# One token tile moved from packed weights to a DMA transpose, and weight pruning by halves, in a 2:4 sparse matmul

## The chip, the cores and the metric

The kernel runs on one core of a Trainium2 chip. The metric is the device time of one execution in microseconds. A profile of one execution lies beside it; times inside it count from the first instruction of its span.

## What is computed

```python
B, S, D = 16, 512, 1024
wg = w.reshape(D // 4, 4, D)                 # groups of 4 rows
mag = abs(wg)
thr = second largest of the 4 magnitudes     # per group and column
mask = (mag >= thr)
wp = (wg * mask).reshape(D, D)               # 2:4 pruned weights
out = einsum("bsd,df->bsf", x, wp) + b       # x is 8192 x 1024, all bf16
```

So the weights are pruned first, two kept of each four rows in a column, and a product of 8192 x 1024 by 1024 x 1024 follows, with a bias.

## The kernel before

**Tiles.** The 8192 tokens are 64 tiles of 128. The product of one tile is 16 matmuls of TensorE (PE) that are 512 columns wide: 8 blocks of 128 input rows by 2 halves of the output columns (h = 0 and 1). `g` = 0 and 1 are the first and the last 512 input rows.

**Weights in pieces.** The weights are loaded in six pieces, numbered from 0: pieces 0 to 3 are 256 columns each of the first input half (g = 0), pieces 4 and 5 are 512 columns each of the second. A partition holds four consecutive rows of the weights, one group, so pruning needs no exchange between partitions. `abs_piece` (L109) makes magnitudes, on VectorE (DVE) except for piece 3, which ScalarE (ACT) does; `prep_piece` (L124) makes maxima and minima of pairs, the threshold, the mask (L150) and the product with the weights (L153). Pieces 0 to 2 do mask and product by halves (two of the four rows each): in pieces 1 and 2 both masks come first, then both products. Piece 3 and later ones take one mask and one product.

**Two ways to use the weights.** While they are still in this *packed* layout, a matmul can read them if the tokens' columns are permuted to match. The first `T` = 8 tiles do so for the first input half: `load_x` (L76) loads half a tile, `transpose_half` (L177) transposes it on PE by four matmuls of 128 columns (L182), `copy_half` (L184, L187) brings it from PSUM to SBUF. These tiles can start on each piece as soon as it is pruned. For the second input half their tokens come transposed by DMA (tile `xg`, L324). All other tiles are transposed wholly by DMA and read the weights in natural order (`wp_nat`), which `unpack` (L170) makes by four DMAs for each piece of 512 columns once it is pruned. The `F` = 6 tiles behind the packed ones are the *fill* tiles: two DMA transposes (L259), one for each input half, bring them to `xfill`; they give PE work between the pieces. The rest comes in batches, one of 2 tiles and then six of 8 (L266).

**The order by hand.** The first part is a string of steps, `FRONT` (L285), and the program keeps the written order on each engine. A step is a letter and numbers:

- `A.i`, `P.i`: magnitudes, then pruning, of piece i.
- `T.t`, `C.t`: PE transpose and ACT copy of packed tile t.
- `M.i.t`: piece i for packed tile t, four matmuls, one for each row m of the groups. `N.i.t.m...` is the same for the listed m alone, so that a half piece can be used. They are 256 columns wide for pieces 0 to 3 and 512 for 4 and 5 (L203).
- `X.q.t`: a fill tile, q = 2g + h, four matmuls of 512 (L203). `Y.t`: a fill tile's h = 1, all eight (L263).
- `V.h.t`: ACT moves a finished half sum to a stage in SBUF (L235). `O.h.t`: DVE adds the second half sum to it (L239). `B`, and the loop's `add_bias`: DVE adds the bias (L243). `evac_dve` (L248) does it straight from PSUM.
- `I`, `D.g`, `G`, `U.g.h`, `Q`, `L.n`: on SP's DMA queue a load of weights, a fill transpose of half g, the transpose to `xg`, an unpack, the bias, a batch's transpose. SP issues them in the order in which they are written.

PSUM has 8 banks, given out in turn (L53), so a sum waits until the one that had its bank has been moved. `later` (L343) holds the stage halves whose bias is added in the main loop, which does the 50 batch tiles (L359).

Of the kernel before, what the change touches and what calls it, by code (L numbers as in the profile page):

```python
# [10 lines left out]
def kernel(  # L11
# [8 lines left out]
    P = 128  # L20
# [7 lines left out]
    B, S, D = x.shape  # L28
# [7 lines left out]
    xf = x.flatten_outer_dims()  # L36
    of = out.flatten_outer_dims()

    T, F = 8, 6
    NE = 8  # L40

    const = ctx.enter_context(tc.tile_pool(name="const", bufs=1))
# [22 lines left out]
    def w_of(i):  # L65
        g, c0, c1 = pieces[i]
        return w_gh[(g, c0 // FH)][:, :, c0 % FH:c0 % FH + c1 - c0]

    def load_w(g, c0, c1, eng=nc.sync, m0=0, m1=4):
        dst = w_gh[(g, c0 // FH)][:, m0:m1, c0 % FH:c0 % FH + c1 - c0]  # L70
        K(eng.dma_start(dst, wv[:, g, m0:m1, c0:c1]))
# [4 lines left out]
    def load_x(ta, tb, eng=nc.sync):  # L76
        xt = const.tile([P, tb - ta, KH], bf16, name=f"xh_{ta}")
        src = xf[ta * P:tb * P, 0:KH].rearrange("(t p) c -> p t c", p=P)
        K(eng.dma_start(xt[:], src))
        for t in range(ta, tb):  # L80
            xh[t] = xt[:, t - ta, :]
# [5 lines left out]
    load_x(4, 5)  # L87
    load_x(5, 6)
    load_w(0, 256, 512)
    load_x(6, 8)  # L90
    load_w(0, 512, 1024)
    bias_sb = const.tile([P, Dout], bf16, name="bias_sb")

# [30 lines left out]
    def prep_piece(i):  # L124
        g, c0, c1 = pieces[i]
        n = c1 - c0
        mag = mags.pop(i)
        magv = mag.rearrange("p (a j) f -> p a j f", j=2)
        hi = tmp.tile([P, 2, FH], bf16, name="hi")[:, :, :n]
        lo = tmp.tile([P, 2, FH], bf16, name="lo")[:, :, :n]  # L130
        for a in ((0, 1), (1, 2)) if i == 0 else ((0, 2),):
            a = slice(*a)
            K(nc.vector.tensor_tensor(hi[:, a], magv[:, a, 0, :], magv[:, a, 1, :], op=Alu.max))  # L133
        K(nc.vector.tensor_tensor(lo, magv[:, :, 0, :], magv[:, :, 1, :], op=Alu.min))  # L134
        t1 = tmp.tile([P, FH], bf16, name="t1")[:, :n]
        t2 = tmp.tile([P, FH], bf16, name="t2")[:, :n]
        K(nc.vector.tensor_tensor(t1, hi[:, 0, :], hi[:, 1, :], op=Alu.min))  # L137
        thr = tmp.tile([P, FH], bf16, name="thr")[:, :n]
        cols = (slice(0, n // 2), slice(n // 2, n)) if i == 0 else (slice(0, n),)
        for c in cols:  # L140
            K(nc.vector.tensor_tensor(t2[:, c], lo[:, 0, c], lo[:, 1, c], op=Alu.max))  # L141
        for c in cols:
            K(nc.vector.tensor_tensor(thr[:, c], t1[:, c], t2[:, c], op=Alu.max))  # L143
        mask = tmp.tile([P, 4, FH], bf16, name="mask")[:, :, :n]

        halves = (slice(0, 2), slice(2, 4)) if i < 3 else (slice(0, 4),)

        def keep(ms, c=slice(0, n)):
            tb = thr[:, None, c].to_broadcast([P, ms.stop - ms.start, c.stop - c.start])
            K(nc.vector.tensor_tensor(mask[:, ms, c], mag[:, ms, c], tb, op=Alu.is_ge))  # L150

        def prune(ms, c=slice(0, n)):
            K(nc.vector.tensor_tensor(w_of(i)[:, ms, c], w_of(i)[:, ms, c], mask[:, ms, c], op=Alu.mult))  # L153

        if i == 0:
            for step in (keep, prune):
                for c in cols:
                    step(halves[0], c)
            keep(halves[1])
            prune(halves[1])  # L160
        else:
            for ms in halves:
                keep(ms)
            for ms in halves:
                prune(ms)
# [100 lines left out]
    def issue_batch(t0, nb):  # L266
# [18 lines left out]
    FRONT = """  # L285
        I.1.0.512 D.0 A.0 P.0 W W W W W W W W W w w T.0 T.1 C.0 T.2 T.3 C.1 T.4 C.2 N.0.0.0 N.0.0.1 T.5
        N.0.1.0 N.0.1.1 N.0.0.2 N.0.0.3 N.0.1.2 N.0.1.3 M.0.2 A.1 C.3 P.1 U.0.0.0.512 I.1.512.1024 G C.4 C.5
        M.0.3 N.0.4.0.1 T.6 T.7 C.6 N.0.4.2.3 C.7 A.2 M.0.5 M.0.6 P.2 M.0.7 N.1.0.0.1 N.1.1.0.1 A.3
        N.1.2.0.1 N.1.0.2.3 N.1.1.2.3 N.1.2.2.3 V.0.0 M.1.3 V.0.1 M.1.4 V.0.2 M.1.5 M.1.6 V.0.3 M.1.7 V.0.4
        P.3 N.2.0.0.1 V.0.5 N.2.1.0.1 N.2.0.2.3 V.0.6 N.2.1.2.3 M.2.2 V.0.7 M.2.3 M.2.4 M.2.5 M.2.6 A.4 P.4  # L290
        U.1.0.0.512 D.1 M.2.7 M.3.0 M.3.1 V.1.0 M.3.2 V.1.1 M.3.3 V.1.2 M.3.4 V.1.3 M.3.5 V.1.4 M.3.6 V.1.5
        M.3.7 V.1.6 X.0.8 V.1.7 X.0.9 V.0.8 X.0.10 V.0.9 X.0.11 V.0.10 X.0.12 V.0.11 X.0.13 V.0.12 V.0.13
        A.5 P.5 U.1.1.0.512 U.0.1.0.512 Q L.0 L.1 N.4.0.0 N.4.1.0 N.4.2.0 N.4.3.0 N.4.0.1 N.4.1.1 N.4.2.1
        N.4.3.1 N.4.0.2 N.4.1.2 N.4.2.2 N.4.3.2 N.4.0.3 N.4.1.3 N.4.2.3 N.4.3.3 M.4.4 O.0.0 M.4.5 O.0.1
        M.4.6 O.0.2 M.4.7 O.0.3 X.2.8 O.0.4 X.2.9 O.0.5 X.2.10 O.0.6 X.2.11 O.0.7 X.2.12 O.0.8 X.2.13 O.0.9
        N.5.0.0 N.5.1.0 N.5.0.1 N.5.1.1 N.5.0.2 N.5.1.2 N.5.0.3 N.5.1.3 O.0.10 O.0.11 O.0.12 O.0.13 M.5.2
        O.1.0 M.5.3 O.1.1 M.5.4 O.1.2 M.5.5 O.1.3 M.5.6 O.1.4 M.5.7 O.1.5 O.1.6 O.1.7 Y.8 B.0.8 Y.9 B.0.9
        Y.10 B.0.10 Y.11 B.0.11 Y.12 B.0.12 Y.13 B.0.13
    """
    for tok in FRONT.split():  # L300
# [8 lines left out]
        elif k == "A":  # L309
            abs_piece(n[0], n[0] == 3)  # L310
        elif k == "P":
            prep_piece(n[0])
        elif k == "T":
            transpose_half(n[0])
# [89 lines left out]
```

## Time and profile before

| | us |
|---|---|
| median of 3 runs | 233.22 (233.02 to 233.74) |
| profiled execution | 233.14 |
| its span, first to last instruction | 231.3 |
| first warm-up matmul (L105) | 0.77 |
| first matmul of a weight piece (L203) | 6.52 |
| first matmul of a fill tile | 21.32 |
| first matmul on unpacked weights of the second input half | 26.50 |
| last fill step (Y) begins the wide block of L263 | 45.49 |
| first batch tile (L369) | 55.85 |

The difference of 1.8 us between the profiled execution's time and its span lies ahead of the first instruction and behind the last. The granted TensorE clock is 0.999 over the span. Up to the batches the order string rules; from there PE runs the same loop body to the end.

### The profile page before, as it was taken

How to read it: one execution, taken by the hardware profiler on the slowest of the kernel's cores; microseconds unless marked ns; L12 is line 12 of the kernel's file. 1: busy time of each engine (PE TensorE's matmuls, PEld its weight loads, DVE VectorE, ACT ScalarE, POOL GpSimd, SP SyncE). 2: the span in 40 equal slices, each digit the busy share in tenths (PEclk: the TensorE clock that was granted, in tenths of full speed). 3: DMA queues.
4: the chain of work that ended last, by engine and by line, in shares of the span. 5: the costliest groups of instructions: out<-in, count | busy, mean ns of one | idle time of the engine just before them, and what ended most of it. 6: DMA issues, size and time to landing. Idle time of an engine off the chain costs nothing.

```text
span 231.3 us, 2789 instructions
## 1 busy us (share of the span) xinstructions
PE 227.9 (99%) x1155; PEld 110.8 (48%) x1155; DVE 120.2 (52%) x213; ACT 18.1 (8%) x33; POOL 0.7 (0%) x6
## 2 busy tenths in 40 slices
PE   8999999999999999999999999999999999999995
PEld 3887444444444444444444444444444444444443
DVE  3999887867997324424424424424424423423434
ACT  2777500000000000000000000000000000000000
POOL 1000000000000000000000000000000000000000
PEclk9999999999999999999999999999999999999999
DMA  6989999999747212991249822695228930122222
GB/s 211 259 188 230 215 191 181 277 263 287 291 181 272 91 73 82 227 302 50 89 116 227 201 95 91 129 256 178 75 91 209 288 137 33 61 91 91 91 93 91
DMA packets 77228, 38.19 MB, mean 165 GB/s; under 512 B 63136, under 2 KB 69024, under 8 KB 77216
## 3 DMA queue, kind: packets, MB, share of 16 engines
q1 hardware_dynamic: 67568, 20.88, 43.5%
q10 hardware_dynamic: 9648, 17.14, 20.0%
q8 instruction: 9, 0.15, 0.3%
q14 instruction: 3, 0.02, 0.0%
HBM read 3.41 MB, written 16.78 MB: 87 GB/s over the span
## 4 chain that ended last, share of the span: by engine, by line
PE 96%; DVE 2%; DMA 1%; issue 0%
PE bank L369 73%; PE bank L203 17%; PE bank L263 6%; DMA w<-in_w_dram 1%; DVE o_last L354 0%; PE bank L182 0%; DVE mag L120 0%; DVE w L153 0%; DVE mask L150 0%; DVE hi L133 0%; DVE lo L134 0%; DVE t L141 0%; DVE thr L143 0%; DVE t L137 0%
## 5 line engine op out<-in xcount | busy, mean ns | idle before, releaser
L369 PE MATMUL bank<-wp_nat,xTb 128*128 128x512 bf16 x752 | 162.5, 379 | 0.0
L248 DVE TENSOR_TENSOR o_pair<-bank,bias_sb 128x512 bf16<-128x512 f32 x104 | 67.3, 687 | 99.6 <-PE bank L369 96.3
L369 PEld LDWEIGHTS <-xTb 128*128 128x128 bf16 x752 | 73.6, 98 | 88.7
L239 DVE TENSOR_TENSOR stage<-bank,stage 128x512 f32<-128x512 f32 x22 | 14.2, 687 | 3.9 <-PE bank L203 3.8
L203 PE MATMUL bank<-w,xT 128*128 128x256 bf16 x128 | 14.6, 273 | 0.0
L203 PE MATMUL bank<-wp_nat,xg 128*128 128x512 bf16 x64 | 14.1, 379 | 0.0
L243 DVE TENSOR_TENSOR o_pair<-stage,bias_sb 128x512 bf16<-128x512 f32 x22 | 14.0, 683 | 0.0
L203 PEld LDWEIGHTS <-xT 128*128 128x128 bf16 x128 | 12.3, 98 | 1.8 <-issue 0.2
L235 ACT COPY stage<-bank 128x512 f32<-128x512 f32 x22 | 11.5, 613 | 3.9 <-PE bank L203 3.9
L203 PE MATMUL bank<-wp_nat,xfill 128*128 128x512 bf16 x48 | 10.7, 379 | 0.0
L263 PE MATMUL bank<-wp_nat,xfill 128*128 128x512 bf16 x48 | 10.5, 379 | 0.0
L203 PEld LDWEIGHTS <-xg 128*128 128x128 bf16 x64 | 6.3, 98 | 7.6
L263 PEld LDWEIGHTS <-xfill 128*128 128x128 bf16 x48 | 4.7, 98 | 5.7
L203 PEld LDWEIGHTS <-xfill 128*128 128x128 bf16 x48 | 4.7, 98 | 5.5
L369 PE MATMUL bank<-wp_nat,xTs 128*128 128x512 bf16 x32 | 7.1, 379 | 0.0
L150 DVE TENSOR_TENSOR mask<-mag,thr 128x512 bf16<-128x512 bf16 (+3 forms) x10 | 5.6, 582 | 0.2
L153 DVE TENSOR_TENSOR w<-w,mask 128x512 bf16<-128x512 bf16 (+3 forms) x10 | 5.6, 581 | 0.1
L105 PE MATMUL bank<-const-bfloat16-1.0 128*128 128x512 bf16 (+1 forms) x11 | 4.2, 569 | 0.8 <-PEq L388 0.8
L369 PEld LDWEIGHTS <-xTs 128*128 128x128 bf16 x32 | 3.1, 98 | 3.8
L187 ACT COPY xT<-bank 128x512 bf16<-128x512 bf16 x8 | 4.1, 606 | 2.9 <-PE bank L182 2.9
L120 DVE TENSOR_SCALAR mag<-w 128x512 uint16<-128x512 uint16 (+2 forms) x6 | 2.7, 467 | 3.0 <-DMA w<-in_w_dram 3.0
L263 PE MATMUL bank<-wp_nat,xTb 128*128 128x64 bf16 (+3 forms) x40 | 3.7, 251 | 0.0
(20 smaller groups left out, 26.4 us busy)
## 6 DMA issues: line engine op xcount, KB each, us to landing
out_dram<-o_pair ACTq DMA_DIRECT2D x25, 512.0 KB, 2.8
out_dram<-o_pair ACTq DMA_DIRECT2D x13, 256.0 KB, 2.1
wp_nat<-w SPq DMA_DIRECT2D x16, 128.0 KB, 2.8
w<-in_w_dram SPq DMA_DIRECT2D x3, 512.0 KB, 6.7
xh<-in_x_dram SPq DMA_DIRECT2D x2, 256.0 KB, 4.2
xh<-in_x_dram ACTq DMA_DIRECT2D x1, 256.0 KB, 4.1
xh<-in_x_dram SPq DMA_DIRECT2D x2, 128.0 KB, 3.9
w<-in_w_dram SPq DMA_DIRECT2D x1, 256.0 KB, 4.3
```

Of the source, the lines that this page charges most:

```text
L105: K(nc.tensor.matmul(bank[7][:, :n], lhsT=ones[:, :P], rhs=ones[:, :n], start=True, stop=True))
L120: K(nc.vector.tensor_single_scalar(mag[:, ms].bitcast(u16), w_of(i)[:, ms].bitcast(u16), 0x7FFF, op=Alu.bitwise_and))
L150: K(nc.vector.tensor_tensor(mask[:, ms, c], mag[:, ms, c], tb, op=Alu.is_ge))
L153: K(nc.vector.tensor_tensor(w_of(i)[:, ms, c], w_of(i)[:, ms, c], mask[:, ms, c], op=Alu.mult))
L187: K(nc.scalar.copy(xt[:], src))
L203: K(nc.tensor.matmul(dst, lhsT=lhs, rhs=rhs, start=c0 == 0 and m == 0, stop=c1 == FH and m == 3))
L235: K(nc.scalar.copy(stage[(h, t)][:], bank[own[(h, t)]][:]))
L239: K(nc.vector.tensor_tensor(st, bank[own[(2 + h, t)]][:], st, op=Alu.add))
L243: K(nc.vector.tensor_tensor(get_o(t)[:, f], stage.pop((h, t))[:], bias_sb[:, f], op=Alu.add))
L248: K(nc.vector.tensor_tensor(get_o(t)[:, f], bank[bk][:], bias_sb[:, f], op=Alu.add))
L263: K(nc.tensor.matmul(bank[bk][:, :c1 - c0], lhsT=xN[t][:, kt, :], rhs=wp_nat[h][:, kt, c0:c1], start=kt == 0, stop=kt == KT - 1))
L369: K(nc.tensor.matmul(bank[bks[h]][:], lhsT=xN[t][:, kt, :], rhs=wp_nat[h][:, kt, :], start=kt == 0, stop=kt == KT - 1))
```

## The change

`T` and `F` become 7 and 7: tile 7 is no longer a packed tile but the first fill tile. Its PE transpose, copy, and its steps M.0.7 to M.5.7 go; X.0.7, X.2.7 and Y.7 with B.0.7 come in. Half of tile 7 is no longer loaded by `load_x`; the fill transposes bring 7 tiles instead of 6, the transpose to `xg` 7 instead of 8. Pieces 1 to 3 do mask, product, mask, product by halves (piece 3 was not halved at all). In the order string the steps on pieces 2 and 3 follow by halves for more tiles: N.2 on tiles 0 to 3 instead of 0 and 1, and N.3 on tiles 0 and 1, where piece 3 had only whole steps.

```diff
-    T, F = 8, 6
+    T, F = 7, 7
...
-    load_x(6, 8)
+    load_x(6, 7)
...
-        halves = (slice(0, 2), slice(2, 4)) if i < 3 else (slice(0, 4),)
+        halves = (slice(0, 2), slice(2, 4)) if i < 4 else (slice(0, 4),)
...
+        elif i < 4:
+            for ms in halves:
+                keep(ms)
+                prune(ms)
         else:
             for ms in halves:
                 keep(ms)
...
-        M.0.3 N.0.4.0.1 T.6 T.7 C.6 N.0.4.2.3 C.7 A.2 M.0.5 M.0.6 P.2 M.0.7 N.1.0.0.1 N.1.1.0.1 A.3
-        N.1.2.0.1 N.1.0.2.3 N.1.1.2.3 N.1.2.2.3 V.0.0 M.1.3 V.0.1 M.1.4 V.0.2 M.1.5 M.1.6 V.0.3 M.1.7 V.0.4
-        P.3 N.2.0.0.1 V.0.5 N.2.1.0.1 N.2.0.2.3 V.0.6 N.2.1.2.3 M.2.2 V.0.7 M.2.3 M.2.4 M.2.5 M.2.6 A.4 P.4
-        U.1.0.0.512 D.1 M.2.7 M.3.0 M.3.1 V.1.0 M.3.2 V.1.1 M.3.3 V.1.2 M.3.4 V.1.3 M.3.5 V.1.4 M.3.6 V.1.5
-        M.3.7 V.1.6 X.0.8 V.1.7 X.0.9 V.0.8 X.0.10 V.0.9 X.0.11 V.0.10 X.0.12 V.0.11 X.0.13 V.0.12 V.0.13
+        M.0.3 N.0.4.0.1 T.6 C.6 N.0.4.2.3 A.2 M.0.5 M.0.6 P.2 N.1.0.0.1 N.1.1.0.1 A.3
+        N.1.2.0.1 N.1.0.2.3 N.1.1.2.3 N.1.2.2.3 V.0.0 M.1.3 V.0.1 M.1.4 V.0.2 M.1.5 M.1.6 V.0.3 V.0.4
+        P.3 N.2.0.0.1 V.0.5 N.2.1.0.1 N.2.2.0.1 N.2.3.0.1 N.2.0.2.3 V.0.6 N.2.1.2.3 N.2.2.2.3 N.2.3.2.3 M.2.4 M.2.5 M.2.6 A.4 P.4
+        U.1.0.0.512 D.1 N.3.0.0.1 N.3.1.0.1 N.3.0.2.3 V.1.0 N.3.1.2.3 M.3.2 V.1.1 M.3.3 V.1.2 M.3.4 V.1.3 M.3.5 V.1.4
+        M.3.6 V.1.5 X.0.7 V.1.6 X.0.8 V.0.7 X.0.9 V.0.8 X.0.10 V.0.9 X.0.11 V.0.10 X.0.12 V.0.11 X.0.13 V.0.12 V.0.13
...
-        M.4.6 O.0.2 M.4.7 O.0.3 X.2.8 O.0.4 X.2.9 O.0.5 X.2.10 O.0.6 X.2.11 O.0.7 X.2.12 O.0.8 X.2.13 O.0.9
+        M.4.6 O.0.2 X.2.7 O.0.3 X.2.8 O.0.4 X.2.9 O.0.5 X.2.10 O.0.6 X.2.11 O.0.7 X.2.12 O.0.8 X.2.13 O.0.9
...
-        O.1.0 M.5.3 O.1.1 M.5.4 O.1.2 M.5.5 O.1.3 M.5.6 O.1.4 M.5.7 O.1.5 O.1.6 O.1.7 Y.8 B.0.8 Y.9 B.0.9
+        O.1.0 M.5.3 O.1.1 M.5.4 O.1.2 M.5.5 O.1.3 M.5.6 O.1.4 O.1.5 O.1.6 Y.7 B.0.7 Y.8 B.0.8 Y.9 B.0.9
```

## Prediction

> **What bounds the kernel now.** The page first: engine shares and the chain of work that ended last.
>
> ```profile
> PE 227.9 (99%) x1155; PEld 110.8 (48%) x1155; DVE 120.2 (52%) x213; ACT 18.1 (8%) x33; POOL 0.7 (0%) x6
> PE 96%; DVE 2%; DMA 1%; issue 0%
> ```
>
> The chain is TensorE (PE) from its first product to the tail. So the question is not which engine is busy, but whether PE's stream, which has no holes now, gets any. A record of a matmul is longer than the distance to the next start, so a hole of 0.1 us can hide in "busy"; I therefore go by start times. Second view, PE's timeline (start, length, line, form, count):
>
> ```profile
> 8.84 0.61 PE L182 MATMUL bank<-ident,xh 128*128 128x128 bf16 x8
> 9.28 12.20 PE L203 MATMUL bank<-w,xT 128*128 128x256 bf16 x110
> 21.32 5.34 PE L203 MATMUL bank<-wp_nat,xfill 128*128 128x512 bf16 x24
> 26.50 7.07 PE L203 MATMUL bank<-wp_nat,xg 128*128 128x512 bf16 x32
> 33.40 5.34 PE L203 MATMUL bank<-wp_nat,xfill 128*128 128x512 bf16 x24
> ```
>
> Prices follow by dividing distances: (9.28-8.84)/8 = 0.056 us a transpose, (21.32-9.28)/110 = 0.109 a matmul of 256 columns, (26.50-21.32)/24 = 0.216 one of 512. The 110 narrow ones stand without a hole. Third view, VectorE (DVE), which makes what they read, at pieces 0 to 3:
>
> ```profile
> 6.38 0.42 DVE L150 TENSOR_TENSOR mask<-mag,thr 128x512 bf16<-128x512 bf16 x1
> 6.83 0.42 DVE L153 TENSOR_TENSOR w<-w,mask 128x512 bf16<-128x512 bf16 x1
> 9.16 0.76 DVE L150 TENSOR_TENSOR mask<-mag,thr 128x512 bf16<-128x512 bf16 x2
> 9.84 0.75 DVE L153 TENSOR_TENSOR w<-w,mask 128x512 bf16<-128x512 bf16 x2
> 10.83 0.43 DVE L120 TENSOR_SCALAR mag<-w 128x1024 uint16<-128x1024 uint16 x1 [0.25 <-DMA w<-in_w_dram]
> 12.82 0.76 DVE L150 TENSOR_TENSOR mask<-mag,thr 128x512 bf16<-128x512 bf16 x2
> 13.50 0.76 DVE L153 TENSOR_TENSOR w<-w,mask 128x512 bf16<-128x512 bf16 x2
> 15.69 0.69 DVE L150 TENSOR_TENSOR mask<-mag,thr 128x1024 bf16<-128x1024 bf16 x1
> 16.41 0.69 DVE L153 TENSOR_TENSOR w<-w,mask 128x1024 bf16<-128x1024 bf16 x1
> 17.02 0.69 DVE L120 TENSOR_SCALAR mag<-w 128x2048 uint16<-128x2048 uint16 x1
> ```
>
> Piece 2 is finished at 14.25 and PE reads its first half from 14.33; piece 3 at 17.11, read from 17.82. PE is thus only 0.1 to 0.7 us behind DVE. Fourth view, SP's queue:
>
> ```profile
> 17.21 5.91 SPq L324 DMA_TRANSPOSE xg<-in_x_dram  x1
> 23.23 2.48 SPq L172 DMA_DIRECT2D wp_nat<-w  x4
> 25.75 3.36 SPq L259 DMA_TRANSPOSE xfill<-in_x_dram  x1
> ```
>
> The first unpack of piece 4 lands at 25.97, read from 26.50.
>
> **The change part by part.**
>
> *Tile 7 changes kind.* PE loses T.7 (4 x 0.056 = 0.22), M.0.7 to M.3.7 (16 x 0.109 = 1.75) and M.4.7, M.5.7 (8 x 0.216 = 1.73); it gains X.0.7, X.2.7, Y.7 (16 x 0.216 = 3.45). Net 0.25 us less work. The place matters more than the net: ahead of N.4.0.0 PE loses 0.22 + 1.75 and gains 0.86, so it has 1.11 us less to do there; behind it, 0.86 more. The copies and adds that go (C.7, V.1.7, one DVE add of 0.69) are off the chain: nothing.
>
> *Mask and product by halves.* Two DVE instructions that don't need each other start 0.34 apart ((13.50-12.82)/2); a product right behind its own mask starts 0.455 behind it (6.38 to 6.83). A piece in the new order: mask 0, product +0.455, mask +0.795, product +1.25, next +1.59. In the old order the second product is at +1.01. So piece 1 or 2 finishes 0.24 later, though its first half is ready 0.22 earlier. Piece 3 takes 1.33 from mask to next instruction now (15.69 to 17.02) and would take 1.59. Bounds for each piece: 0 (the dependent start costs no more than the free one) and 0.25; I take the upper, since the row at 6.83 is the same form in the same order.
>
> DVE's times then, by adding. Piece 1: second product 10.41 to 10.83; the next instruction could start at 10.75. It waits for a load today (idle 0.25 before 10.83). That load has 128 KB less ahead of it, and the 256 KB load before it needed 1.12 us (landings 7.01 to 8.13), so it should land some 0.5 earlier than its 10.81; I take 10.75. Piece 2: mask 12.74, products end 13.61 and 14.41. Piece 3: mask 15.84, products end 16.72 and 17.51. Piece 4 starts 0.41 late and its product ends at 22.68 + 0.41 = 23.09.
>
> *PE against that.* A matmul that waited for a product started 0.05 behind the product's end (7.26 to 7.31). M.0.6 comes 0.22 earlier, but tile 6's copy still ends at 9.87: M.0.6 at 9.92, N.1.0.0 at 10.36, its products long done. N.2.0.0: 28 narrow matmuls on, 13.41; product 13.66, **0.25 waited**. 28 narrow ones later 16.72, product 16.77, **0.05**. Four later 17.21; the second half of piece 3 comes at 17.57, **0.36**. From there nothing on DVE holds PE: 24 narrow (2.62) and 28 wide (6.04) bring N.4.0.0 to 26.23, against 26.50 now. Behind it 0.86 more work: **+0.59 us** at the end. The other way round: -0.25 for the work, +0.66 for these waits and +0.21 for M.0.6 give +0.62. I take +0.6.
>
> *Queues.* The transpose for the fill tiles has 28 blocks of 128 x 128 instead of 24 (512 more packets of 256 B, at some 1,130 per us while one runs: 0.45), but the load ahead is shorter by as much: the unpack of piece 0/1 stays near its 13.04, and X.0.7, which reads it at 20.2, has over 1 us. G shrinks by 4 blocks (0.45 to 0.6). So U.1.0 is no longer held by G (23.13) but by piece 4's product (23.09): issued near 23.2, landed near 25.9 as now. N.4.0.0 at 26.23 has 0.3 left of the 0.52 it has today; its next three parts are 0.65 apart, PE needs them 0.86 apart. If that cover went, each us of lateness beyond 0.3 would be a us of time. D.1 is 0.45 longer: 15 of its 16 parts land at 31.15 today, so near 31.6; X.2.7 reads it at 26.23 + 28 x 0.216 = 32.27. Later issues (U.1.1, the bias, L.0, L.1) come up to half a us later; the first batch lands at 41.86 and is read from 55.85. The PSUM banks that are reused sooner (N.2.1.0 behind V.0.0, X.0.8 behind V.1.0) have over 1 us each by ScalarE's 0.5 us per copy (8 copies in 4.01).
>
> **The sum.** The profiled execution took 233.14 us: span 231.3 and 1.8 around it. With 0.6 it is 233.74; the median of the three runs lies 0.08 higher, so 233.8. That is 0.26% up, within the 0.3% (0.7 us) below which a measurement of this kernel can't tell a change from none.
>
> **Rivals.**
>
> *Order is free on DVE.* If a dependent start cost no more than a free one, pieces 1 to 3 would end as fast as now, and with the earlier load 0.33 earlier; piece 3 would end at 16.79, N.2 and N.3 would hardly wait, N.4.0.0 would come at 25.57 and the end at -0.93 + 0.86 = -0.07: 233.15. It needs the unpack to come by 25.5 too. Against it: 0.455 and 0.34 stand side by side at 6.38 to 7.18. The Trainium skill, VectorE: DVE Perf Modes, section The DRAIN you can't avoid, says that the next operation starts only when the pipe is empty and that a semaphore after each costs nothing extra; by that this rival would be the forecast. This trace differs: the second mask starts 0.08 us before the first one's record ends, the dependent product 0.03 after. Chance 0.11.
>
> *PE is never held.* Only the saved work counts: -0.25, 232.97. It needs piece 3's second half by 16.4, before even the old kernel has it. Chance 0.04.
>
> *Slower: the second fill transpose lands late.* Today its 16th part lands at 32.68, 1.5 us behind the other 15; the first one's too (16.54 against 15.04), while G's 16 parts lie within 0.13. In both a 16,384-byte packet on queue q8 (at 14.49 and 30.45, 1.0 and 1.2 us long) falls into the last blocks. These packets come every 27.6 us later on, which is 128 wide matmuls and their 128 weight loads, so they follow PE's count of instructions. If one falls into D.1 again, it lands at 31.15 + 0.45 + 1.53 = 33.1, X.2.7 waits 0.9, and the end is +1.5: 234.7. It decides from a landing after 32.27. Against it: PE issues 16 matmuls fewer ahead of N.4, so the packet comes some 3.2 us later, at 33.6, when D.1 is down. The Trainium skill, Runtime: NRT & Kernel Launch, section Instruction fetch mechanics, has engines refill their instructions in blocks of 16 KiB, 256 instructions, at a cost mostly hidden; the size agrees with q8, and hidden holds for PE but not for the transpose beside it. A late U.1.0 gives the same sign. Chance 0.25 for this side.
>
> **How the numbers follow.** Forecast 0.60, own range 233.4 to 234.2; a bit over a quarter of it lies above 0.3%, as a w load that lands at 10.83 alone adds 0.08. Faster by over 0.3% only in the tail of the second rival: 0.03. Within 0.3%: the rest of the first two rivals 0.12 and 0.44 of the forecast, 0.56. Slower: 0.16 and 0.25, 0.41. The range reaches from just above the second rival to the third: 233.0 to 234.8.
>
> **What would show it.** DVE rows with products 0.45 behind masks, piece 3's second product ending near 17.5; narrow matmuls broken by gaps before N.2 and inside N.3; the wide block at 20.2; N.4.0.0 near 26.2, and Y.7 near 44.4 (26.23 + 84 x 0.216). No gap at N.3, or one at N.4.0.0 or X.2.7 above 0.2, would make the prediction wrong.

## The result, and the profile after

The changed kernel takes 233.57 us in the median of 22 runs, the kernel before 233.02 beside it: a ratio of 1.0024 (95% interval 1.0016 to 1.0033), 0.55 us or 0.24% slower. The profiled execution of the changed kernel is one of its slower ones: 234.25 us with a span of 232.4, against 233.14 and 231.3 before. So its profile shows about twice the loss of the median; where the other half comes from is the first question for the experiments.

First the page of the changed kernel, engine shares and chain.

```profile
PE 227.2 (98%) x1123; PEld 110.3 (47%) x1143; DVE 120.4 (52%) x214; ACT 17.1 (7%) x31; POOL 0.7 (0%) x6
PE 90%; DVE 3%; DMA 3%; SPq 1%; issue 1%
```

PE has 90% of the chain instead of 96%: DVE and the DMA that loads the weights stand in it with 3% each, against 2% and 1%. (20 matmul records are missing here, seen from the 1143 weight loads; a gap of exactly one matmul in every 50 is such a hole in the records and no wait.) PE's timeline of the changed kernel (start, length, line, form, count, idle before and who ended it):

```profile
9.06 4.51 PE L207 MATMUL bank<-w,xT 128*128 128x256 bf16 x38
14.16 3.71 PE L207 MATMUL bank<-w,xT 128*128 128x256 bf16 x32 [0.59 <-DVE w L153]
18.07 2.78 PE L207 MATMUL bank<-w,xT 128*128 128x256 bf16 x24 [0.20 <-DVE w L153]
20.68 6.21 PE L207 MATMUL bank<-wp_nat,xfill 128*128 128x512 bf16 x27
26.73 5.99 PE L207 MATMUL bank<-wp_nat,xg 128*128 128x512 bf16 x27
32.77 6.21 PE L207 MATMUL bank<-wp_nat,xfill 128*128 128x512 bf16 x28
```

The block of 110 narrow matmuls is broken in two places: N.2.0.0 at 14.16 and N.3's second halves at 18.07, both released by products of DVE. The idle figures are short by the modelled ends; by start times the waits are 0.75 and 0.36, a further 0.06 lies ahead of N.3.0.0, and 0.19 ahead of M.0.6 at 9.90. The fill tiles begin 0.64 earlier than before, yet N.4.0.0 comes 0.23 later. DVE in the same stretch:

```profile
8.96 0.42 DVE L150 TENSOR_TENSOR mask<-mag,thr 128x512 bf16<-128x512 bf16 x1
9.42 0.42 DVE L153 TENSOR_TENSOR w<-w,mask 128x512 bf16<-128x512 bf16 x1
9.76 0.42 DVE L150 TENSOR_TENSOR mask<-mag,thr 128x512 bf16<-128x512 bf16 x1
10.21 0.42 DVE L153 TENSOR_TENSOR w<-w,mask 128x512 bf16<-128x512 bf16 x1
11.24 0.43 DVE L120 TENSOR_SCALAR mag<-w 128x1024 uint16<-128x1024 uint16 x1 [0.60 <-DMA w<-in_w_dram]
13.22 0.42 DVE L150 TENSOR_TENSOR mask<-mag,thr 128x512 bf16<-128x512 bf16 x1
13.68 0.43 DVE L153 TENSOR_TENSOR w<-w,mask 128x512 bf16<-128x512 bf16 x1
17.59 0.42 DVE L153 TENSOR_TENSOR w<-w,mask 128x512 bf16<-128x512 bf16 x1
```

A product starts 0.46 behind its mask, the next mask 0.34 behind that product. But piece 2 starts at 11.24 instead of the forecast 10.75: DVE stood idle for 0.60 until the load of weight columns 512 to 1023 had landed, at 11.21 (a load has landed when the last of its 16 parts is down). This is *the load* from here on. That load has 128 KB less ahead of it than before and still lands 0.4 later. SP's queue of the changed kernel:

```profile
18.06 5.57 SPq L328 DMA_TRANSPOSE xg<-in_x_dram  x1
23.73 2.48 SPq L176 DMA_DIRECT2D wp_nat<-w  x4
26.26 3.66 SPq L263 DMA_TRANSPOSE xfill<-in_x_dram  x1
```

The unpack of piece 4 is issued at 23.73, 0.14 behind piece 4's product (23.59) and 0.10 behind G; its first part lands at 26.50, so N.4.0.0 did not wait for it.

### The profile page after: what moved, and what is told of

Same layout as the page of the kernel before. It is cut to its first block, busy times and chain, and to the rows that moved or that the text cites. A ratio compares the mean times of both kernels' runs of the same rounds, so it can differ in the third digit from the quotient of the medians.

```text
span 232.4 us, 2743 instructions
## 1 busy us (share of the span) xinstructions
PE 227.2 (98%) x1123; PEld 110.3 (47%) x1143; DVE 120.4 (52%) x214; ACT 17.1 (7%) x31; POOL 0.7 (0%) x6
## 4 chain that ended last, share of the span: by engine, by line
PE 90%; DVE 3%; DMA 3%; SPq 1%; issue 1%
PE bank L373 72%; PE bank L207 12%; PE bank L267 6%; DMA w<-in_w_dram 3%; SPq L79 1%; DVE w L153 1%; DVE mask L150 1%; SPq L71 0%; DVE o_last L358 0%; DVE hi L133 0%; DVE lo L134 0%; DVE thr L143 0%; DVE mag L120 0%; DVE t L141 0%; DVE t L137 0%
## 5 line engine op out<-in xcount | busy, mean ns | idle before, releaser
L252 DVE TENSOR_TENSOR o_pair<-bank,bias_sb 128x512 bf16<-128x512 f32 x105 | 68.0, 687 | 101.2 <-PE bank L373 95.4
L207 PE MATMUL bank<-w,xT 128*128 128x256 bf16 x112 | 13.3, 273 | 0.8 <-DVE w L153 0.8
L207 PE MATMUL bank<-wp_nat,xfill 128*128 128x512 bf16 x55 | 12.4, 379 | 0.1
L267 PE MATMUL bank<-wp_nat,xfill 128*128 128x512 bf16 x55 | 12.2, 379 | 0.1
L207 PE MATMUL bank<-wp_nat,xg 128*128 128x512 bf16 x54 | 12.1, 380 | 0.1
L207 PEld LDWEIGHTS <-xT 128*128 128x128 bf16 x112 | 10.7, 98 | 2.7 <-issue 1.1
L267 PEld LDWEIGHTS <-xfill 128*128 128x128 bf16 x56 | 5.5, 98 | 6.6
L207 PEld LDWEIGHTS <-xg 128*128 128x128 bf16 x56 | 5.5, 98 | 6.6 <-issue 0.2
L207 PEld LDWEIGHTS <-xfill 128*128 128x128 bf16 x56 | 5.5, 98 | 6.4
L153 DVE TENSOR_TENSOR w<-w,mask 128x512 bf16<-128x512 bf16 (+2 forms) x11 | 5.9, 546 | 0.3
L150 DVE TENSOR_TENSOR mask<-mag,thr 128x512 bf16<-128x512 bf16 (+2 forms) x11 | 5.9, 543 | 0.2
```

Of the source, the lines that this page charges most:

```text
L207: K(nc.tensor.matmul(dst, lhsT=lhs, rhs=rhs, start=c0 == 0 and m == 0, stop=c1 == FH and m == 3))
L252: K(nc.vector.tensor_tensor(get_o(t)[:, f], bank[bk][:], bias_sb[:, f], op=Alu.add))
L267: K(nc.tensor.matmul(bank[bk][:, :c1 - c0], lhsT=xN[t][:, kt, :], rhs=wp_nat[h][:, kt, c0:c1], start=kt == 0, stop=kt == KT - 1))
```

## The experiments

**Theory:** with 7 packed tiles PE has less *cover*, that is less work of its own to do while a piece is being pruned, so it stands still until DVE has piece 2 and piece 3, and what makes DVE late makes the kernel late. **Rivals:** the order of mask and product is the cost by itself; or the longer fill transpose and its queue are. All kernels were timed beside the kernel before on the same chip.

**A second profile of the changed kernel** (no edit).

> The changed kernel once more, for a second profile: the one on record is of an execution of 234.25 us, 0.7 above this kernel's median, and in it the load of weight columns 512 to 1023 lands at 11.21 (10.81 in the kernel before), so that piece 2 starts late. Theory (PE is held by pieces 2 and 3, since it has 1.1 us less to do ahead of them): about 0.6 over the kernel before. In a profile with the load down by 10.75, PE waits some 0.25 ahead of N.2 and 0.36 inside N.3; each 0.1 that the load is later adds 0.1 to the first wait and moves the rest along. Rival (the longer fill transpose makes the load late, and that is the loss): the load lands at 11.2 again, and the wait ahead of N.2 is 0.75 again.

1.0042 (1.0029 to 1.0055; 234.04 us, 1.00 over the kernel before in the median of 5 runs), more than in the 22 runs, though the two intervals overlap (the first ended at 1.0033).

```profile
13.98 3.71 PE L207 MATMUL bank<-w,xT 128*128 128x256 bf16 x32 [0.69 <-DVE w L153]
```

The load landed at 11.03, the wait ahead of N.2 was 0.85 by start times, the others 0.06 and 0.36. A late load was thus no accident of one execution: both profiles of the changed kernel have it, and no run gave a profile of one of its 233.4 us executions. Theory and rival both live on.

**The order alone**, on 8 packed tiles.

```diff
-        halves = (slice(0, 2), slice(2, 4)) if i < 3 else (slice(0, 4),)
+        halves = (slice(0, 2), slice(2, 4)) if i < 4 else (slice(0, 4),)
...
+        elif i < 4:
+            for ms in halves:
+                keep(ms)
+                prune(ms)
```

> The kernel before, with mask, product, mask, product by halves in pieces 1 to 3 and nothing else: 8 packed tiles, the old order string. Theory: DVE finishes piece 3 some 0.4 to 0.5 later (17.5 to 17.6 instead of 17.1), which PE's 17.8 for the first matmul on piece 3 still covers, and N.2's second half at 14.77 covers piece 2 (14.5): no wait, within 0.1 of the kernel before. Rival (the order of mask and product is what costs): 0.4 to 0.6 slower.

1.0002 (0.9993 to 1.0011). PE's timeline of that kernel:

```profile
11.74 9.55 PE L207 MATMUL bank<-w,xT 128*128 128x256 bf16 x86
21.12 5.34 PE L207 MATMUL bank<-wp_nat,xfill 128*128 128x512 bf16 x24
26.30 1.46 PE L207 MATMUL bank<-wp_nat,xg 128*128 128x512 bf16 x6
```

The narrow block has no hole: piece 3's last product runs from 17.01 to 17.43, and 8 tiles' matmuls cover it. N.4.0.0 is at 26.30. The order costs nothing where there is cover; that it alone makes the loss is ruled out.

**The tile alone**: the changed kernel with the old order (the diff above taken back).

> The changed kernel with the old order of mask and product: masks first in pieces 1 and 2, piece 3 in one mask and one product. 7 packed tiles and the new order string stay. Theory: the wait ahead of N.2 stays as it is (the first half of piece 2 is ready at the same time: piece 1 ends 0.24 earlier, the half 0.22 later), piece 3 is whole by 16.8 to 17.1 and PE waits 0.1 for it instead of 0.4: 0.2 to 0.4 over the kernel before, 0.2 to 0.3 under the changed one; PE may then meet the unpack of piece 4 as its next wait. Rival of the order: as fast as the kernel before less 0.25. Rival of the transposes: as slow as the changed kernel, 0.6.

1.0025 (1.0014 to 1.0036; 233.71). Slower than the kernel before, but not measurably faster than the changed one: a miss in size.

```profile
13.89 6.41 PE L203 MATMUL bank<-w,xT 128*128 128x256 bf16 x56 [0.18 <-DVE w L153]
```

The wait for piece 3 shrank as expected (0.14 instead of 0.42 in all), but N.2.0.0 came later: 3.15 behind the load's landing (13.89 and 10.74), 2.95 in the changed kernel (14.16 and 11.21). The expectation took piece 1's end as what starts piece 2; here the load started it (10.76, DVE idle 0.24), so masks first only made the first half 0.2 later. N.4.0.0 came 15.44 behind the load's landing, against 15.52 with the new order: 0.08, all that the order is worth where the load starts piece 2.

**All first halves of piece 3 ahead of the second ones.**

```diff
-        N.3.0.0.1 N.3.1.0.1 N.3.0.2.3 V.1.0 N.3.1.2.3 M.3.2 V.1.1 M.3.3 ... M.3.6 V.1.5
+        N.3.0.0.1 N.3.1.0.1 ... N.3.6.0.1 N.3.0.2.3 V.1.0 N.3.1.2.3 V.1.1 ... N.3.6.2.3 V.1.5
```

> The changed kernel with all seven tiles' first halves of piece 3 (14 narrow matmuls) ahead of any second half, instead of two tiles' (4). Theory: the wait of 0.36 inside N.3 goes, since 10 more matmuls (1.09 us) stand ahead of it; N.4.0.0 then comes near 25.85 and meets the unpack of piece 4 (landed near 25.9 to 26.5): 0.2 to 0.4 under the changed kernel where the unpack is in time, less where it is not, and a new wait of up to 0.4 ahead of N.4.0.0. Rival (the loss lies at the queues, not at DVE's halves): no change against the changed kernel.

```profile
14.05 6.33 PE L207 MATMUL bank<-w,xT 128*128 128x256 bf16 x56 [0.36 <-DVE w L153]
20.21 6.21 PE L207 MATMUL bank<-wp_nat,xfill 128*128 128x512 bf16 x28
26.37 3.83 PE L207 MATMUL bank<-wp_nat,xg 128*128 128x512 bf16 x17
```

All 56 narrow matmuls of pieces 2 and 3 stand together: the wait inside N.3 is gone. From 20.21, 28 wide ones end at 26.25; N.4.0.0 starts at 26.37, 0.12 later, behind the unpack that landed at 26.23. So part of the gain went to the next wait. N.4.0.0 stands 15.27 behind the load, 0.25 better than in the changed kernel. The time, 1.0038 (1.0025 to 1.0051), can't show 0.25 beside a load that landed at 11.10 in this profile.

**The fill transpose later**, to get the load through.

```diff
-        I.1.0.512 D.0 A.0 ... U.0.0.0.512 I.1.512.1024 G
+        I.1.0.512 A.0 ... U.0.0.0.512 D.0 I.1.512.1024 G
```

> The changed kernel with the first fill transpose issued behind the unpack of pieces 0 and 1 (from about 13.4) instead of at 5.4. In four profiles so far with 7 packed tiles the load of weight columns 512 to 1023 landed at 10.74 to 11.21, with 8 at 10.62 and 10.81, though it has 128 KB less ahead of it; packets of the fill transpose run from 9 on, while 7 of the load's 16 parts are still out. Theory (the transpose's packets beside it make the load's last parts late, which makes DVE late, which PE now waits for): the load lands by 10.3, DVE starts piece 2 near 10.75 or as soon as piece 1 is done, the wait ahead of N.2 is 0.2 to 0.3 instead of 0.5 to 0.85, and the time falls 0.3 to 0.6 against the changed kernel: 0.3 to 0.6 over the kernel before. Rival (the load is late for another reason): lands at 10.7 to 11.2 as now, no change. The fill tiles' data should land by 18.5 and is needed at 20.2.

1.0063 (1.0050 to 1.0075): the time is a miss on the wrong side, the early landing a hit. The load landed at 9.60. In the stretch from 7 to 9 us the DMA engines moved 333 GB/s, against 235 in the changed kernel (last column; the row with the earlier transpose first):

```profile
7.00:9.00 2.00, 2.00 (x24) 1.79 (x22) 1.90 (x7) 1.49 (x4) 0.00 (x0) 1.00 0.97 235
```

```profile
7.00:9.00 2.00, 2.00 (x22) 1.83 (x21) 1.85 (x6) 1.52 (x4) 0.00 (x0) 1.00 1.02 333
```

And PE in the run with the later transpose:

```profile
13.58 3.71 PE L207 MATMUL bank<-w,xT 128*128 128x256 bf16 x32 [0.22 <-DVE w L153]
17.49 2.78 PE L207 MATMUL bank<-w,xT 128*128 128x256 bf16 x24 [0.20 <-DVE w L153]
21.20 6.22 PE L207 MATMUL bank<-wp_nat,xfill 128*128 128x512 bf16 x27 [0.93 <-DMA xfill<-in_x_dram]
```

N.2's wait fell to 0.38, piece 2 now starting when piece 1 is done (10.67). In its place came a wait of 1.09 for the fill tiles, landed at 21.15 instead of the 18.5 that was expected.

**The same with N.3's halves first.**

> The changed kernel with both: the first fill transpose later, and all first halves of piece 3 ahead of the second ones. If both theories hold, PE has only the wait ahead of N.2 (0.25) and the copy of tile 6, and meets the unpack of piece 4 next: N.4.0.0 at 25.8 to 26.0 and 0.1 to 0.3 over the kernel before, the best one can do with 7 packed tiles here. If the load is late for another reason: as the run with the halves alone, 0.9 over.

1.0064 (1.0052 to 1.0076). The load landed at 9.71, the fill tiles at 20.82 with a wait of 1.19: what N.3 gave back was spent waiting for them.

**Loads ahead of the fill transpose**, a middle place for it.

```diff
-        I.1.0.512 D.0 A.0 ... U.0.0.0.512 I.1.512.1024 G
+        I.1.0.512 I.1.512.1024 D.0 A.0 ... U.0.0.0.512 G
```

> The changed kernel with the load of weight piece 5 (512 KB) issued ahead of the first fill transpose, so that the transpose's packets start some 2 us later, but not as late as in the run that put it behind the unpack (there the load of columns 512 to 1023 landed at 9.60 and 9.71, and the fill tiles at 20.8 to 21.15, which cost 1.1). Theory: that load lands at 9.6 to 10.2, the wait ahead of N.2 is 0.25 to 0.4, the one inside N.3 stays 0.36, the fill tiles' data lands by 19 and holds nobody: 0.5 to 0.6 over the kernel before, steadily, without the executions at 234. Rival (a wait takes its place): the fill tiles, the unpack of pieces 0 and 1 or the next transpose are late for X.0.7 or N.4 by 0.5 or more, 1 us over.

1.0026 (1.0016 to 1.0036; 233.47 us): the median is 0.48 over the kernel before, as expected, but not steadily, for 234.33 and 234.48 are among the 10 executions. The profile is of the one at 234.48 and does not show what was expected: the load landed at 11.46, piece 2 started as late as ever, the wait ahead of N.2 was 1.14, and 255 GB/s moved from 7 to 9. The transpose's own packets began only at 10.60. At 9.60, when the whole load was down in the run with the later transpose, 5 of its 16 parts were still out here. So the load is late without those packets beside it; that theory falls in this form. No profile shows one of the faster executions. What the runs with early landings (9.60, 9.71) share is that neither the transpose nor a second load was queued on SP behind the loads until they were down.

**The same with N.3's halves first.**

> The same with all first halves of piece 3 ahead of the second ones. Theory: only the wait ahead of N.2 is left; N.4.0.0 at 25.7 to 25.9 unless the unpack of piece 4 is later; 0.1 to 0.3 over the kernel before, and not faster than it: N.4.0.0 would have to come by 25.63 for that (26.50 less the 0.86 of work moved behind it). Rival: as above, 1 us over.

1.0022 (1.0012 to 1.0032; 233.42 us), the lowest of the kernels with 7 packed tiles, though not measurably below the changed one, and 0.43 over the kernel before where 0.1 to 0.3 was expected. Its load landed at 10.74, before the transpose's first packet (11.18), and N.4.0.0 started at 25.92, at the late end of what was expected. It would have had to come by 25.63 to tie with the kernel before.

**Tile 7's half still loaded.**

```diff
-    load_x(6, 7)
+    load_x(6, 8)
```

> The changed kernel, but tile 7's half is still loaded with tile 6's (256 KB as before), and not used. Theory (the fill transpose beside it makes the load late): the packets ahead of the load don't decide; it lands at 10.8 to 11.5 and the time is that of the changed kernel or up to 0.4 more. Rival (the shorter load ahead itself, for instance its other shape, makes the next one late): it lands at 10.6 to 10.8 as in the kernel before, and the time falls by 0.2 to 0.4.

1.0040 (1.0027 to 1.0053; 233.71). The profile has the load at 10.65 and 233.69 us: the changed kernel with an early load.

```profile
13.60 3.71 PE L207 MATMUL bank<-w,xT 128*128 128x256 bf16 x32 [0.31 <-DVE w L153]
17.50 2.78 PE L207 MATMUL bank<-w,xT 128*128 128x256 bf16 x24 [0.19 <-DVE w L153]
...
26.16 1.67 PE L207 MATMUL bank<-wp_nat,xg 128*128 128x512 bf16 x7
```

The landing is the rival's; the time isn't lower than the changed kernel's two. One landing between the others can't tell theory and rival apart: undecided. But the three profiles show the price of a late load: landings 0.38 and 0.56 later than here (11.03 and 11.21) go with executions 0.35 and 0.56 longer (234.04 and 234.25).

**More loaded ahead, on 8 and on 7 packed tiles**, `load_x(6, 9)` in both.

> The kernel before (8 packed tiles), with one tile's half (128 KB) loaded in addition and not used, in the same DMA as tiles 6 and 7, ahead of the load of columns 512 to 1023. That load should land 0.3 to 0.6 later than 10.6 to 10.8, at 10.9 to 11.4. Theory (8 packed tiles give PE about 0.4 us of cover here: piece 2's first half is ready at 13.97 for a matmul at 14.33): a landing up to 11.2 costs nothing, 11.4 costs 0.2; within 0.2 of the kernel before. Rival (late loads cost the same in both kernels): 0.3 to 0.6 slower.

> The changed kernel with two tiles' halves (256 KB) loaded in addition and not used, in tile 6's DMA, so that as much stands ahead of the load of columns 512 to 1023 as in the run beside it. Theory (no cover with 7 packed tiles: N.2.0.0 starts 2.95 behind that load's landing): at 10.9 to 11.4 the profiled execution takes 233.69 plus the landing's distance from 10.65, so 233.9 to 234.5, 0.4 to 0.6 more over the kernel before than the run beside it. Rival (a late load costs nothing here): 233.5.

8 tiles: 1.0005 (0.9994 to 1.0015); 7 tiles: 1.0038 (1.0025 to 1.0052; profile 233.84). The lever failed: with 384 KB in that DMA the load landed at 10.46 and 10.82, not later than with 128 or 256 KB, so 8 tiles were not put to the test by a late load. On 7 tiles the rule of the expectation (233.69 + 0.17 = 233.86) gave the time to 0.02, although the wait had moved: tile 6's transpose waited 0.8 for its longer load, and N.2 waited no more. DVE's piece 3 set the same end.

**Five matmuls added in the waits.**

```diff
+        elif k == "H":
+            for _ in range(n[0]):
+                K(nc.tensor.matmul(bank[n[1]][:, :256], lhsT=ones[:, :P], rhs=ones[:, :256], start=True, stop=True))
...
-        P.3 N.2.0.0.1 V.0.5 ... N.3.0.0.1 N.3.1.0.1 N.3.0.2.3
+        P.3 H.2.7 N.2.0.0.1 V.0.5 ... N.3.0.0.1 N.3.1.0.1 H.3.6 N.3.0.2.3
```

> The changed kernel with five extra matmuls of 256 columns on a bank that is free then, which change no output: two ahead of N.2.0.0 and three ahead of N.3's second halves. They are 5 x 0.109 = 0.55 us of PE work. Theory (PE stands still there, 0.25 or more and 0.36): they fill the waits and cost nothing, within 0.1 of the changed kernel. Rival (PE's stream as a whole is the bound there and the loss lies elsewhere): 0.55 more than the changed kernel.

233.89 us, 1.0036 (1.0023 to 1.0048): between the two measurements of the changed kernel (1.0024 and 1.0042). The rival's 0.55 more would be 1.0048 or above, the upper end of the interval, so the time speaks against it but the trace has to decide.

```profile
13.59 0.38 PE L313 MATMUL bank<-const-bfloat16-1.0 128*128 128x256 bf16 x2
13.82 3.65 PE L207 MATMUL bank<-w,xT 128*128 128x256 bf16 x32
17.31 0.49 PE L313 MATMUL bank<-const-bfloat16-1.0 128*128 128x256 bf16 x3
17.64 2.78 PE L207 MATMUL bank<-w,xT 128*128 128x256 bf16 x24
```

PE runs through without an idle moment, with 0.55 us of useless work in it; N.4.0.0 is 15.69 behind the load, 0.17 more than without. So about 0.4 of the 0.55 was free. In this execution PE itself was late at N.2 (M.0.6 at 10.09 instead of 9.90), so the rest fits a hole that was smaller. The waits are real.

**Profiles side by side.** The eight whose PE order and DVE order are those of the kernel before or of the changed kernel, or differ from the kernel before in DVE's order alone; the other six took further steps there or made PE wait for the fill tiles. Times in us; "first" is the first matmul on pruned weights, "rest" is from N.4.0.0 to the end of the span.

| kernel | packed tiles | load landed | first | N.4.0.0 | rest |
|---|---|---|---|---|---|
| before | 8 | 10.81 | 6.52 | 26.50 = first + 19.98 | 204.85 |
| order alone | 8 | 10.62 | 6.33 | 26.30 = first + 19.98 | 204.84 |
| more loaded | 8 | 10.46 | 6.38 | 26.36 = first + 19.98 | 204.84 |
| changed | 7 | 11.21 | 6.65 | 26.73 = load + 15.51 | 205.70 |
| changed, again | 7 | 11.03 | 6.24 | 26.55 = load + 15.52 | 205.71 |
| half kept | 7 | 10.65 | 6.24 | 26.16 = load + 15.52 | 205.71 |
| more loaded | 7 | 10.82 | 6.33 | 26.34 = load + 15.52 | 205.71 |
| loads first | 7 | 11.46 | 6.37 | 26.97 = load + 15.51 | 205.72 |

This is the case in one table. With 8 packed tiles N.4.0.0 follows PE's own first matmul by a constant, whenever the load lands between 10.46 and 10.81 (no later landing was seen there); with 7 it follows the load by a constant and does not care when PE began. The rest is 0.86 longer in all kernels with 7. The constant behind the load holds as long as the load, not piece 1, starts piece 2 (piece 1 lets DVE go between 10.47 and 10.67 in the profiles with 7 tiles and the new order).

## Why the prediction came out as it did

The forecast was +0.6 by PE waiting for DVE, and the time went up by 0.55. The mechanism is shown; that the size came so close is in part luck, since the step on the load was wrong. Its steps:

- *Prices of PE's work.* 0.86 more behind N.4.0.0: measured 0.86. Right.
- *DVE's order.* Product 0.455 behind its mask, 0.24 to 0.25 later per piece: the rows show 0.46 and 0.34, and from piece 2's first instruction to piece 3's last product 6.78 (11.24 to 18.02), predicted 6.76. Right, and the first rival (order is free on DVE) falls with it. A dependent start costs 0.12 us more than a free one here. The Trainium skill, VectorE: DVE Perf Modes, section The DRAIN you can't avoid, has the next operation wait for an empty pipe with or without a semaphore, and adds that one that is not held starts earlier. The trace shows both kinds of start, and differs by those 0.12 us. DVE's later pieces reach the end only where DVE is waited for: 0.00 on 8 tiles, about 0.08 in the comparison on 7.
- *Waits.* M.0.6 predicted 0.21, measured 0.19; N.3 0.05 and 0.36, measured 0.06 and 0.36. Right. N.2 predicted 0.25: 0.75, 0.85, 0.47 and 0.38 in profiles with the load at 11.21, 11.03, 10.65 and 9.60.
- *The load: wrong.* "I take 10.75" for piece 2's start, with the load "some 0.5 earlier than its 10.81". In the changed kernel and its neighbours with the transpose early it landed between 10.6 and 11.5. The step failed in reasoning from bytes ahead: 128, 256 and 384 KB in the DMA ahead gave landings of 10.61 to 11.21, 10.62 to 10.81, and 10.46 to 10.82, so fewer bytes did not bring it earlier. The prediction priced a late load at 0.08 for 10.83 and had the slope right (0.1 for 0.1), but not the spread. This is why the profiled execution lost 1.1: 0.86 behind N.4.0.0 and 0.23 ahead of it.
- *The size: in part luck.* The same kernel measured again lost 1.00. The median's 0.55 would follow from N.4.0.0 about 0.3 earlier than before, near the forecast's 0.27, which means piece 2 started near 10.55. Nine of the 22 executions lie together at 233.37 to 233.46; their spans of 231.6 to 231.7, less the 205.71 of the table, put N.4.0.0 at 25.9 to 26.0. An estimate from the run with the half kept: DVE could have gone on at 10.47, 0.34 behind the start of piece 1's last product at 10.13, and N.4.0.0 stands 15.49 behind piece 2's start there, so a load down by then gives 25.96. No profile of the changed kernel shows such an execution; that the typical load is earlier than the profiled ones is inferred, not shown.
- *Queues.* The unpack behind piece 4's product, N.4.0.0 not held by it: right, with 0.23 left (0.3 forecast). The 0.65 between its parts is the distance of their issues; in the changed kernel they landed 0.35 to 1.04 apart, still in time for PE. The issue of U.0.0 "near its 13.04" came at 13.89, 0.85 late, hidden behind X.0.7 as forecast.
- *The slower rival.* It asked whether a 16,384-byte packet of queue q8 meets the second fill transpose. It moved from 30.45 to 33.50 (forecast 33.6); the transpose's 16 parts landed within 31.82 and 31.96, where the 16th had come 1.5 us behind the others before, and X.2.7 at 32.77 did not wait. In the kernel before exactly 256 PE instructions, matmuls and weight loads together, start between one such packet and the next, five times running from 82.93 on. Measured from N.4.0.0 the packet moved from 3.95 to 6.77, which is 13 wide matmuls with their weight loads where 16 were counted. The Trainium skill, Runtime: NRT & Kernel Launch, section Instruction fetch mechanics, has blocks of 256 instructions. The trace agrees that the packet follows PE's instructions, in the loop to the last one, in the first part nearly. The slower side did come in single executions (234.22 to 234.51, three of 22); in the one that was profiled it came by the load, which the rivals did not name.

The rival of the longer fill transpose and its queue has no wait of its own: in the changed kernel X.0.7, N.4.0.0 and X.2.7 start without a gap, so those transfers act at most through the landing of the load.

What stays open: why the load lands late when the transpose, or another load, is queued early. Moving the transpose from 5.4 to 14.4 is the only edit that brought it to 9.6 (9.71 in the second such run). Whether the issuing itself, the lead that some DMA engines take over others, or traffic beside it does that was not separated.

No kernel here beat the one before. With 7 packed tiles the best profile had N.4.0.0 at 25.92, and 25.63 would be a tie with the profiled execution of the kernel before.

## What to carry to other kernels

Work that is saved ahead of a producer's chain is saved only if the producer is early by as much; here PE had 1.1 us less to do ahead of DVE's pieces and 0.86 more behind them, and DVE's schedule became the time. Before taking cover away, look for what the cover was hiding, and price the spread of the loads that start the chain, not one landing: with cover the spread seen here cost nothing, without it the later landings were in the time one for one. To see which one binds, set one event (here N.4.0.0) against each candidate start over several profiles; the binding one is a constant away.

## What the runs showed of the hardware beyond that

- The last of a load's 16 parts can be far behind the others: in the changed kernel 15 parts of the load were down by 10.08 and the 16th by 11.21.
- From 7 to 9 us, ahead of nearly all of the fill transpose's packets (the earliest ran at 8.98), the DMA engines moved 333 and 336 GB/s in the two profiles with no transpose or further load queued behind the loads of pieces 2 to 4, and 232 to 310 GB/s in the twelve with one queued.
- A DMA transpose held SP's queue until some 12 of its blocks of 128 x 128 were left: 1,488 to 1,607 packets of 256 bytes, in twelve transposes of four profiles (the kernel before, the changed kernel, the half kept, the transpose later). So the fill transpose issued at 5.38 kept the queue until 12.90 before and until 13.76 in the changed kernel.
- A 16,384-byte packet of queue q8 beside a transpose's last blocks went with one late part: in the kernel before, 15 parts of the second fill transpose were down by 31.15 and the 16th by 32.68, with the packet at 30.45; in the changed kernel, with the packet at 33.50, all were down within 31.82 and 31.96.
